# Attention on one core: GpSimd's background work at the end of a head step, memory terms two pieces later, reciprocals in two parts

## The chip, the core and the metric

One Trainium2 chip; the kernel runs on one of its cores. The metric is the device time of one execution in microseconds. Three runs of the kernel before took 708.51, 709.81 and 711.28 us (median 709.81). The profiled execution took 709.86 us, with a span of 708.2 us from its first to its last instruction.

The names of engines: PE is TensorE (PEld its weight load), DVE is VectorE, ACT is ScalarE, POOL is GpSimd, SP is SyncE, which here only issues DMAs. Each engine works through its own instructions in the order in which the program lists them, so an instruction that waits holds back all that stand behind it on that engine.

## What is computed

Two independent halves, side by side in the output. Half B is a spectral filter (a two-dimensional FFT, a product with weights, the inverse FFT); the change doesn't touch it. Half A is attention over 4 segments of 512 tokens with 32 heads of width 18, each segment with its own softmax and with a memory of the segments before:

```python
for s in range(N):                       # N = 4 segments
    qs, ks, vs = q[:, :, s], k[:, :, s], v[:, :, s]
    logits = jnp.einsum("bhqd,bhkd->bhqk", qs, ks) * scale + mask
    p = _softmax(logits, axis=-1)
    a_dot = jnp.einsum("bhqk,bhkd->bhqd", p, vs)
    pq = phi(qs)
    num = jnp.einsum("bhld,bhde->bhle", pq, M)
    den = jnp.einsum("bhld,bhd->bhl", pq, z)[..., None] + 1e-6
    a_mem = num / den
    o = g * a_mem + (1.0 - g) * a_dot
    outs.append(o)
    M = M + jnp.einsum("bhld,bhle->bhde", phi(ks), vs)
    z = z + jnp.einsum("bhld->bhd", phi(ks))
# o of all segments, (S, D) @ wo
```

The scores are large, so the kernel works them with high precision: operands are split into high and low parts, and the row maxima are subtracted inside the matmul.

## The kernel before, in words

The program lists FFT, projections of q, k and v, and the inverse FFT first (to about 355 us); the rest, function `attention`, is what the change works in. The order of its instructions is written out by hand: Python generators are advanced a piece at a time, and each piece lists a few instructions.

**Head steps.** The main loop runs t = 0 to 132, and step t handles one head of one segment (128 heads in all). Eight steps share a stack of q and k (`Qs`, `Ks`, loaded by four DMAs each, `stack_dmas`); the q of stack n+2 is loaded from step 8n on. Step t lists `s1(t+11)`, three pieces that compute scores for the maxima of a head eleven steps ahead (PE L656, L669; DVE reads them from PSUM: L670 `mx`, L664 `junk`, three PSUM banks "s1"), and `s2(t)`, three pieces that compute the scores again with the maxima subtracted (PE L705, L709/L710, L714) and their exponentials on ACT (L706, L711, L715). Every second step has half a `pv` (PE L734), the product with v for a quad of four heads. At the last head of a quad, GpSimd sets the masked corners of the four heads' exponentials to zero (`sel`, POOL L719), and the `pv` of that quad, two steps later, needs them.

**Maxima of a quad.** `mpath(k+2)` starts at the end of step t with t%4 == 0: GpSimd splits the quad's 128 x 16 maxima into a high and a low part (`mh`, POOL L685, L686), PE transposes them in step t+1 (`mt`, L689, behind that step's `pv`), ACT copies them and sends them to `Qs` by a DMA.

**Background.** `run_bg(0)` early in a step and `run_bg(1.2)` later in it advance the generators in the list `bg`, one after the other; with the rate of 1.2 this makes six turns in five steps, so in every fifth step there are two. The list holds, in order: `late_setup` (loads the output weights `wo` in six parts through two buffers `ob`; ACT rounds the high part `woh`, GpSimd makes the low part `wol`, L628), and for each segment g = 1, 2, 3 then `mixed(g)`, a part of the output projection of the segment before (`oproj`, PE L877), `den(g+1)` and the rest of `oproj`. `later(k, f)` puts f at the end of a later step: with k = 1 it is listed at the end of the same step, behind the step's `mpath`, lanes and U copies.

**`mixed(g)`** interleaves two things over five tiles of heads, in the order `ORD`. `combine(g-1)` finishes the segment before: PE spreads the reciprocal row sums over the rows (`pb`, L854), DVE multiplies (L857, L859), for a segment with memory GpSimd adds the memory term (`am`, L860), ACT rounds the high part (`oh`, L839), and GpSimd makes the low part (`ol`, L844). From step 118 on DVE takes the place of GpSimd in both (`s.now>=117`). `mem1(g, t)` makes the memory term of segment g: PE `pn` (L807), ACT copies it into `am` (L809), and in the next turn PE `pb` with the reciprocal denominators (L813) and DVE's product (L814). Up to there all these matmuls write the one PSUM bank "post". `mem1` starts d = 4 turns behind `combine` (d = 5 for g = 3).

**Reciprocals.** `recip` runs in the `lane` list, one piece a step: load 128 x 128 row sums (or denominators), wait three steps, reciprocal on DVE (L760), one step later ACT and GpSimd split it into three bf16 parts (L762 to L766), then a store to and a load from DRAM on SP give the wide copy `rr` (or `rd`) that `pb` needs. It runs eight times: for the row sums `rD` of segments 0 to 2 and the denominators `dD` of segments 1 to 3 with `slack=2`, and twice at the end for segment 3 without slack.

**The end.** Behind step 132 a loop runs what is left of `bg` (the projection of segment 2) and, at its turns 3, 8 and 10, `last_tile` (PE L886, DVE L887) for segment 3; then comes the projection of segment 3 (`last_proj`, L906).

Of the kernel before, what the change touches and what calls it, by code (L numbers as in the profile page):

```python
# [5 lines left out]
F32=mybir.dt.float32; F32R=mybir.dt.float32r  # L6
# [381 lines left out]
class ATT:  # L388
# [222 lines left out]
    def late_setup(s,cp):  # L611

        nc,io=s.nc,s.io; q=[]
        s.sel=cp.tile([96,5,126],BF,name="sel",bufs=1); nc.gpsimd.dma_start(s.sel,io["sel"].rearrange("p (t m) -> p t m",t=5))
        s.woh=cp.tile([128,5,576],F32R,name="woh",bufs=1); s.wol=cp.tile([128,5,576],F32R,name="wol",bufs=1)
        for t in (0,1,2,3,5,4,6):
            if t: yield
            if t<6:
                x=cp.tile([128,576],F32,name="ob"); q.append((t,x))
                nc.sync.dma_start(x,io["wo"][:,576*t:576*t+576])  # L620
            yield
            if t!=5: yield
            if len(q)>(t<6):
                u,x=q.pop(0)
                if u==5: nc.scalar.copy(s.wol[64:96,4],x[64:96]); continue
                r=128 if u<4 else 72
                nc.scalar.copy(s.woh[:,u],x)
                nc.gpsimd.tensor_tensor(s.wol[:r,u],x[:r],s.woh[:r,u].bitcast(F32),op=OP.subtract)  # L628
        yield
        yield from s.gates()  # L630
    def stack_dmas(s,n,qk):
# [120 lines left out]
    def recip(s,src,dst,gate,eps,load,slack=0):  # L752
        nc=s.nc; tp=s.tp
        w=tp.tile([128,3,128],BF,name="rw",bufs=2); y=tp.tile([128,128],F32,name="ry",bufs=2)
        nc.sync.dma_start(y,src.rearrange("h (b c) -> (h b) c",b=4))
        yield
        yield
        yield
        if eps: nc.vector.tensor_scalar(y,y,1e-6,None,op0=OP.add)
        nc.vector.reciprocal(y,y)  # L760
        yield
        nc.scalar.activation(y,y,AF.Copy,scale=gate)  # L762
        nc.scalar.copy(w[:,0],y)
        nc.gpsimd.tensor_tensor(y,y,w[:,0],op=OP.subtract)
        nc.gpsimd.tensor_copy(w[:,1],y)
        nc.gpsimd.tensor_tensor(w[:,2],y,w[:,1],op=OP.subtract)  # L766
        for _ in range(slack): yield
        nc.sync.dma_start(bass.AP(tensor=dst.tensor,offset=dst.offset,ap=[[128,128],[32*512,3],[1,128]]),w)
        yield
        yield  # L770
        r=tp.tile([96,512],BF,name=load,bufs=1)
        nc.sync.dma_start(r,dst)
        s.rc[load]=r
        yield
# [42 lines left out]
    def mixed(s,g):  # L817

        c=s.combine(g-1)
        d=5 if g==3 else 4  # L820
        for i in range(5+d):
            next(c,None); yield
            if i>=d:
                for _ in s.mem1(g,ORD[i-d]): yield
# [4 lines left out]
    def combine(s,g):  # L829

        nc=s.nc; tp=s.tp; xs=s.ux
        s.oh=[None]*5; s.ol=[None]*5
        eng=lambda: nc.vector if s.now>=117 else nc.gpsimd
        yield
        yield
        def high(u):
            r=126 if u<4 else 72
            s.oh[u]=tp.tile([128,512],F32R,name="oh",bufs=5); s.ol[u]=tp.tile([128,512],F32R,name="ol",bufs=5)
            (nc.vector.tensor_copy if s.now>=119 else nc.scalar.copy)(s.oh[u][:r],s.am[u][:r])  # L839
        def low(u):  # L840
            r=126 if u<4 else 72
            A,B=s.oh[u],s.ol[u]
            l=B if u<4 else tp.tile([128,512],F32R,name="ol4",bufs=1)
            eng().tensor_tensor(l[:r],s.am[u][:r],A[:r].bitcast(F32),op=OP.subtract)  # L844
            if u==4:
                s.later(1,lambda: nc.sync.dma_start(B[:72].bitcast(F32),A[:72].bitcast(F32)))
                s.later(2,lambda: (nc.sync.dma_start(A[72:128].bitcast(F32),l[:56].bitcast(F32)),nc.sync.dma_start(B[72:88].bitcast(F32),l[56:72].bitcast(F32))))
        late=g==2
        for t in range(7+late):
            if t>1 and not late: high(ORD[t-2]); low(ORD[t-2])  # L850
            if t<5:
                i=t; t=ORD[t]; r=126 if t<4 else 72; x=xs[t]
                pb=s.post("pb")
                nc.tensor.matmul(pb[:r],s.sel[:,t,:r],s.rc["rr"],start=True,stop=True)  # L854
                if g==0:
                    s.am[t]=tp.tile([126,512],F32,name="am",bufs=5)
                    nc.vector.tensor_tensor(s.am[t][:r],x[:r],pb[:r],op=OP.mult)  # L857
                else:
                    nc.vector.tensor_tensor(x[:r],x[:r],pb[:r],op=OP.mult)  # L859
                    eng().tensor_tensor(s.am[t][:r],x[:r],s.am[t][:r],op=OP.add)  # L860
                t=i
                if t<2: s.later(1,lambda t=t: s.ux_load(g,ORD[t+3]))
            if late and 1<t<7: high(ORD[t-2])
            if late and t>2: low(ORD[t-3])
            yield
# [290 lines left out]
```

## Time and profile before

| What | us |
|---|---|
| median of three runs | 709.81 |
| profiled execution | 709.86 |
| its span | 708.2 |
| TensorE busy | 678.8 |
| DVE busy | 544.8 |
| ACT busy | 455.8 |
| GpSimd busy | 194.6 |
| GpSimd's masks, L719, 132 instructions | 78.5 |
| GpSimd's low parts of the weights, L628, 5 instructions, each | 1.41 |
| GpSimd's low parts `ol`, L844, 10 instructions, each | 1.27 |

A row of the profile names the line of the kernel, the engine, the operation, what it writes and reads, how often (x), and what ended the idle time of the engine before it (`<-`). A window row gives the length of a stretch, the busy time of PE, PEld, DVE, ACT and POOL in it with the number of instructions, the granted TensorE clock (1.00 is full), the share of the time in which the 16 DMA engines were busy, and GB/s. A PE that is busy need not be working at its peak rate.

### The profile page before, as it was taken

The page shows a single profiled execution, that of the slowest core. Times are in us where ns is not written, and L with a number is a line of the kernel's source. Part 1 is how long each engine was busy: PE and PEld are TensorE (multiplying, and loading weights), DVE is VectorE, ACT ScalarE, POOL GpSimd, SP SyncE. Part 2 cuts the span into 40 slices and gives each one's busy share as a digit, 9 for nine tenths or more (in the row PEclk, how much of TensorE's full clock was granted, in tenths as well). Part 3 has the DMA queues.
Part 4 walks back from the last instruction along what each step waited for, and adds up shares of the span by engine and source line. Part 5 has one row for each costly group of instructions (what it writes and reads, how often), then busy time and mean ns, then how long its engine had stood idle before and what let it go on. Part 6 is the DMA issues. An engine that isn't in the chain of part 4 may idle for free.

```text
span 708.2 us, 14408 instructions
## 1 busy us (share of the span) xinstructions
PE 678.8 (96%) x4991; PEld 501.3 (71%) x4991; DVE 544.8 (77%) x1258; ACT 455.8 (64%) x1004; POOL 194.6 (27%) x392
## 2 busy tenths in 40 slices
PE   4999999999999999999999899999999999998997
PEld 3999769879779879998954454445566445663587
DVE  4899969899699789797787787988657876567533
ACT  3777796585686484544388777777656776567421
POOL 3111000100200102665135333444233752235310
PEclk9999999999999999999999999999999999999999
DMA  9897355666384679999338976976766766442151
GB/s 328 256 305 202 115 141 187 186 185 202 100 250 156 178 196 311 202 240 267 100 114 210 190 163 143 207 182 167 154 129 181 182 166 154 92 122 65 29 164 74
DMA packets 71146, 123.80 MB, mean 175 GB/s; under 512 B 12184, under 2 KB 39174, under 8 KB 67482
## 3 DMA queue, kind: packets, MB, share of 16 engines
q1 hardware_dynamic: 64422, 106.89, 57.4%
q0 software_dynamic: 5632, 15.76, 8.2%
q8 instruction: 39, 0.64, 0.4%
q10 hardware_dynamic: 1020, 0.25, 0.2%
q14 instruction: 33, 0.27, 0.1%
HBM read 82.10 MB, written 39.81 MB: 172 GB/s over the span
## 4 chain that ended last, share of the span: by engine, by line
PE 68%; DMA 8%; ACT 4%; DVE 4%; POOL 2%; issue 2%; SPq 0%; ACTq 0%; DVEq 0%; POOLq 0%
PE pj L464 12%; PE pv L734 9%; PE s L656 9%; PE pjv L464 8%; PE po L877 6%; PE i L309 3%; PE i L298 3%; PE s L705 3%; PE s L709 2%; DMA yb<-yout 2%; PE pn L807 2%; PE s L669 2%; PE pm L532 2%; PE s L714 2%; DMA Ks<-qkD 1%
## 5 line engine op out<-in xcount | busy, mean ns | idle before, releaser
L664 DVE CUSTOM_DVE_ANT_0 junk<-s,x 128x512 bf16<-128x512 f32 x248 | 137.0, 552 | 58.0 <-PE s L656 52.6
L719 POOL TENSOR_SCALAR_AFFINE_SELECT P<-P 128x512 f32<-128x512 f32 (+2 forms) x132 | 78.5, 626 | 112.9 <-ACT P L706 104.1
L670 DVE TENSOR_REDUCE mx<-s 128x4 f32<-128x512 f32 x128 | 87.7, 685 | 5.6 <-PE s L669 3.7
L706 ACT ACTIVATE P<-s 128x512 f32<-128x512 f32 x128 | 77.7, 607 | 10.8 <-PE s L705 3.8
L734 PE MATMUL pv<-P,vs 128*32 128x512 f32 (+3 forms) x1024 | 82.5, 439 | 0.1
L715 ACT ACTIVATE P<-s 128x256 f32<-128x256 f32 x128 | 49.8, 389 | 46.1 <-PE s L714 45.7
L711 ACT ACTIVATE P<-s 128x512 f32<-128x512 f32 x128 | 77.4, 605 | 2.4 <-PE s L710 2.2
L656 PE MATMUL s<-Ks,Qs 108*128 108x384 bf16 (+3 forms) x256 | 69.1, 301 | 1.5 <-DMA ux<-uD 1.0
L734 PEld LDWEIGHTS pv<-P,vs 128*32 128x32 f32 x1024 | 26.9, 109 | 45.3 <-issue 35.1
L464 PE MATMUL pj<-x,wqkh 128*128 128x512 f32 x162 | 56.5, 409 | 0.0
L208 DVE TENSOR_TENSOR Z<-t,t 128x290 f32<-128x290 f32 (+1 forms) x96 | 48.4, 553 | 0.1
L656 PEld LDWEIGHTS <-Qs 108*128 108x128 bf16 x320 | 31.5, 98 | 23.5 <-issue 12.1
L208 DVE TENSOR_TENSOR t<-Z 128x580 f32<-128x580 f32 x64 | 46.1, 755 | 0.0
L669 PE MATMUL s<-tri,idb 128*128 128x128 bf16 x256 | 43.0, 219 | 0.0
L522 POOL MEMSET vt<- 128x32 f32 x16 | 2.3, 162 | 141.3 <-PE pm L532 119.5
L298 PE MATMUL i<-civ,Y 128*128 128x256 f32 (+1 forms) x288 | 39.3, 289 | 0.2 <-POOL Y L283 0.2
L298 PEld LDWEIGHTS i<-civ,Y 128*128 128x128 f32 (+1 forms) x288 | 36.5, 181 | 1.0 <-POOL Y L283 0.4
L309 PE MATMUL i<-itab,T 128*128 128x290 f32 (+1 forms) x224 | 36.7, 306 | 0.5 <-DVE yout L317 0.4
L464 PE MATMUL pj<-x,wqkl 128*128 128x512 f32 x90 | 35.6, 395 | 0.0
L464 PE MATMUL pj<-xh,wqkl 128*128 128x512 f32 x90 | 35.5, 395 | 0.0
L143 PE MATMUL f<-ftab,eh 128*128 128x290 f32 x128 | 25.3, 321 | 10.7 <-DMA ftab<-ftab 10.6
L464 PE MATMUL pj<-xh,wqkh 128*128 128x512 f32 x90 | 35.5, 395 | 0.0
(210 smaller groups left out, 1806.3 us busy)
## 6 DMA issues: line engine op xcount, KB each, us to landing
qkD<-sp SPq DMA_DIRECT2D x32, 384.0 KB
xin<-xb SPq DMA_DIRECT2D x16, 384.0 KB
cfw<-cfw POOLq DMA_DIRECT2D x16, 384.0 KB, 4.7
civ<-civ POOLq DMA_DIRECT2D x16, 384.0 KB, 9.0
vs<-vD SPq DMA_DIRECT2D x16, 330.0 KB
vD<-vt SPq DMA_DIRECT2D x16, 311.0 KB
W<-w SPq DMA_DIRECT2D x16, 290.0 KB
yb<-yout SPq DMA_DIRECT2D x16, 290.0 KB
```

The source lines that it names most:

```text
L208: v.tensor_tensor(o,a,b,op=op)
L298: nc.tensor.matmul(p[:m,k],Y[i][:,q,c*128:c*128+m],cc[:,hl,o:o+256],start=n==0,stop=n==5)
L309: nc.tensor.matmul(p,x,t,start=n==0,stop=n==6)
L464: s.nc.tensor.matmul(out,a,b,start=i==0,stop=i==len(L)-1)
L656: nc.tensor.matmul(out,Q[:108,h,128*i:128*i+128],K[:108,h,:128*(i+1)],start=True,stop=True)
L664: nc.vector.tensor_tensor_reduce(out=junk[:,:w],in0=src,in1=s.mask[:,512-w:],scale=1.0,scalar=-3.0e38, op0=OP.add,op1=OP.max,accum_out=s.m ...
L669: nc.tensor.matmul(pa[:,o+w-128:o+w],s.idb,s.tri,start=False,stop=True,skip_group_check=True)
L670: nc.vector.tensor_reduce(out=s.mx[k][:,hh],in_=pa.rearrange("p (b c) -> p b c",c=128),axis=mybir.AxisListType.X,op=OP.max)
L706: nc.scalar.activation(P[0][:,hh],p0,AF.Exp,scale=SC)
L711: nc.scalar.activation(P[1][:,hh],p1,AF.Exp,scale=SC)
L719: nc.gpsimd.affine_select(out=x[:,r],in_=x[:,r],pattern=[[0,r.stop-r.start],[1,128]],compare_op=OP.is_ge,fill=0.0,base=0,channel_multiplie ...
L734: nc.tensor.matmul(s.pvt[32*hh:32*hh+32,128*j:],vt[:,j,19*h:19*h+32],mv[0][:,hh,mv[1]],start=j==0,stop=j>1,skip_group_check=True)
```

## The change

Four places, all in half A:

1. `late_setup`: GpSimd's low part of an output weight is listed at the end of its step (`later(1, ...)`), and a `yield` follows, so that the generator takes one more turn for each of five parts.
2. `recip`: with slack, except for the row sums of segment 2, the reciprocal is made in two halves of 64 columns, with a step between them. What follows in `recip` comes one step later.
3. `mixed`: for g = 1 and 2, `mem1` starts 6 turns behind `combine` and no longer 4, so `mixed` takes 21 turns and no longer 19.
4. `combine`: GpSimd's addition of the memory term and its low part are listed at the end of the step, if the step is one in which a quad's maxima are split (t%4 == 0, which at that place is `s.now%4 == 3`), for segments 0 and 1.

```diff
                 nc.scalar.copy(s.woh[:,u],x)
-                nc.gpsimd.tensor_tensor(s.wol[:r,u],x[:r],s.woh[:r,u].bitcast(F32),op=OP.subtract)
+                s.later(1,lambda u=u,x=x,r=r: nc.gpsimd.tensor_tensor(s.wol[:r,u],x[:r],s.woh[:r,u].bitcast(F32),op=OP.subtract))
+                yield
...
         if eps: nc.vector.tensor_scalar(y,y,1e-6,None,op0=OP.add)
-        nc.vector.reciprocal(y,y)
+        if slack and src is not s.rD[2]:
+            nc.vector.reciprocal(y[:,:64],y[:,:64])
+            yield
+            nc.vector.reciprocal(y[:,64:],y[:,64:])
+        else: nc.vector.reciprocal(y,y)
...
         c=s.combine(g-1)
-        d=5 if g==3 else 4
+        d=5 if g==3 else 6
...
-            eng().tensor_tensor(l[:r],s.am[u][:r],A[:r].bitcast(F32),op=OP.subtract)
+            x=s.am[u]; f=lambda e=eng(): e.tensor_tensor(l[:r],x[:r],A[:r].bitcast(F32),op=OP.subtract)
+            f() if eng() is nc.vector or s.now%4<3 or g==2 else s.later(1,f)
...
-                    eng().tensor_tensor(s.am[t][:r],x[:r],s.am[t][:r],op=OP.add)
+                    f=lambda t=t,x=x,r=r,e=eng(): e.tensor_tensor(s.am[t][:r],x[:r],s.am[t][:r],op=OP.add)
+                    f() if eng() is nc.vector or s.now%4<3 or g==2 else s.later(1,f)
```

## The prediction

> **What bounds the kernel now.** I read the page first, then the windows of the attention stage, then the idle times of TensorE in order of time.
>
> ```profile
> span 708.2 us, 14408 instructions
> PE 678.8 (96%) x4991; PEld 501.3 (71%) x4991; DVE 544.8 (77%) x1258; ACT 455.8 (64%) x1004; POOL 194.6 (27%) x392
> 355.00:395.00 40.00, 37.43 (x336) 19.47 (x338) 33.39 (x98) 32.07 (x77) 18.42 (x31) 1.00 0.70 166
> 550.00:590.00 40.00, 38.42 (x313) 19.29 (x306) 32.00 (x93) 29.20 (x68) 23.81 (x34) 1.00 0.78 178
> 635.00:670.00 35.00, 32.25 (x265) 14.40 (x257) 23.49 (x48) 22.60 (x53) 15.88 (x28) 1.00 0.19 54
> ```
>
> The columns of a window are its length, the busy times of PE, PEld, DVE, ACT and POOL, the granted clock, the DMA share and GB/s. TensorE is busy in all but 29.4 us of 708.2, so nothing here can be worth more than a few per cent. The three stretches are the ones the change works in; together they hold 2.57 + 1.58 + 2.75 = 6.9 us of idle TensorE.
>
> More is lost than these idle times show, because a late matmul also stretches its neighbours. So I cut windows at the starts of successive L705 matmuls: each is one head step, and its length is the first column. The first three are quiet steps (with a maxima transpose and pv; short; with pv). Then a step with one memory matmul pair (pn), one with a broadcast (pb), one with half an output projection, and then steps that the change touches: 9, 13, 17, 44, 86, 89, 91, 116.
>
> ```profile
> 432.18:434.82 2.64, 2.64 (x28) 1.25 (x27) 2.13 (x9) 1.89 (x6) 0.42 (x2) 1.00 0.26 56
> 434.82:436.10 1.28, 1.28 (x14) 0.82 (x11) 1.20 (x4) 1.24 (x4) 0.00 (x0) 1.00 0.52 146
> 436.10:438.69 2.59, 2.59 (x30) 1.20 (x28) 2.11 (x8) 1.73 (x5) 1.39 (x3) 1.00 0.64 152
> 577.58:579.72 2.14, 2.14 (x16) 1.17 (x14) 1.68 (x6) 1.78 (x5) 0.98 (x1) 1.00 0.41 123
> 567.70:569.14 1.44, 1.44 (x14) 0.92 (x12) 1.24 (x4) 1.40 (x5) 0.00 (x0) 1.00 0.91 149
> 631.62:633.85 2.23, 2.23 (x20) 1.75 (x18) 1.73 (x6) 2.09 (x6) 0.64 (x1) 1.00 0.00 0
> 371.51:374.71 3.20, 2.82 (x30) 1.16 (x28) 2.37 (x10) 1.92 (x6) 2.54 (x6) 1.00 0.92 205
> 379.91:383.45 3.54, 3.03 (x29) 1.13 (x27) 2.31 (x10) 1.92 (x6) 2.88 (x7) 1.00 0.95 273
> 388.60:392.23 3.63, 2.81 (x30) 1.25 (x28) 2.36 (x10) 2.69 (x8) 2.19 (x4) 1.00 1.00 200
> 446.74:449.33 2.59, 1.56 (x13) 0.85 (x11) 2.45 (x7) 2.56 (x8) 1.90 (x5) 1.00 0.72 158
> 555.89:559.05 3.16, 2.56 (x16) 1.20 (x14) 2.49 (x8) 2.24 (x6) 2.84 (x3) 1.00 0.74 196
> 563.48:567.70 4.22, 3.76 (x32) 1.54 (x30) 2.87 (x11) 2.64 (x8) 2.87 (x4) 1.00 0.99 186
> 569.14:573.34 4.20, 3.87 (x33) 1.71 (x30) 3.06 (x10) 2.26 (x6) 2.43 (x2) 1.00 0.68 135
> 640.31:642.28 1.97, 1.47 (x11) 0.83 (x9) 1.95 (x5) 1.73 (x4) 1.42 (x3) 1.00 0.01 2
> ```
>
> So pn costs 2.14 - 1.28 = 0.86, pb 0.16, half a projection 0.95. What a step takes over its parts: step 9 3.20 - 2.64 = 0.56, step 13 0.90, step 17 0.99, step 44 2.59 - 1.28 = 1.31, step 86 3.16 - (1.28 + 0.86 + 0.16) = 0.86, step 89 4.22 - (2.64 + 0.86) = 0.72, step 91 4.20 - (2.59 + 0.86 + 0.16) = 0.59, step 116 1.97 - (1.28 + 2 x 0.16) = 0.37. What ended the idle time says whose they are:
>
> ```profile
> 391.71 0.23 PE L689 MATMUL mt<-idb,mh 128*128 128x128 bf16 x1 [0.82 <-POOL mh L686]
> 398.09 0.32 PE L656 MATMUL s<-x,Qs 108*128 108x384 bf16 x1 [0.95 <-DVE mg L664]
> 448.99 0.32 PE L656 MATMUL s<-Ks,Qs 108*128 108x384 bf16 x1 [1.03 <-DMA ux<-uD]
> 557.57 0.65 PE L807 MATMUL pn<-pq,Mst 72*72 72x512 f32 x1 [0.60 <-DVE ux L859]
> 567.18 0.23 PE L689 MATMUL mt<-idb,mh 128*128 128x128 bf16 x1 [0.46 <-POOL mh L686]
> 641.85 0.38 PE L854 MATMUL pb<-rr,sel 96*126 96x512 bf16 x1 [0.50 <-DVE ux L859]
> 644.89 0.23 PE L689 MATMUL mt<-idb,mh 128*128 128x128 bf16 x1 [0.44 <-POOL mh L686]
> 680.68 0.38 PE L886 MATMUL pb<-rr,sel 96*126 96x512 bf16 x1 [0.77 <-DVE ux L887]
> ```
>
> **The change part by part.** Counting the yields (the background gets six turns in five head steps) gives the order of every queue.
>
> (a) *Low parts of the output weights.* Same five instructions, issued at the step's end, one more turn each. On GpSimd now:
>
> ```profile
> 386.62 2.40 POOL L719 TENSOR_SCALAR_AFFINE_SELECT P<-P 128x512 f32<-128x512 f32 x4 [3.74 <-ACT P L706]
> 389.81 1.41 POOL L628 TENSOR_TENSOR wol<-ob,woh 72x576 fp32r<-72x576 f32 x1 [0.79 <-ACT woh L627]
> 391.16 0.20 POOL L685 CAST mh<-mg 128x16 bf16<-128x16 f32 x1
> ```
>
> The split of the maxima (mh) stands behind a 1.41 us low part that itself waits for ScalarE. Moved, they land in steps 5, 8, 11, 14 and 20; the splits of steps 8, 16 and 20 come ahead of theirs, and only step 11's stays between the masks and a split, issued earlier than step 16's was. That frees 0.56 + 0.90 + 0.99 = 2.45 us. But step 20's end waits for the next heads' Qs, which the matmul at 398.09 is the first to use (idle 0.95). The DMA engines at that time, the last of the four Qs parts on SP, and one weight load:
>
> ```profile
> 386.00:388.00 2.00, 2.00 (x27) 0.99 (x18) 1.65 (x6) 1.86 (x6) 1.38 (x3) 1.00 0.55 139
> 388.00:398.00 10.00, 8.33 (x77) 4.16 (x75) 8.18 (x28) 7.69 (x20) 4.78 (x9) 1.00 1.01 200
> 389.31 0.37 SPq L640 DMA_DIRECT2D Qs<-reD  x1
> ob<-wo SPq DMA_DIRECT2D x6, 288.0 KB
> ```
>
> From 388 to 398 the DMA engines are full (1.01). Issue can move earlier by the 1.46 us of steps 9 and 13, but only 0.9 us (45% of 386 to 388) was free; and the later turns put the last 288 KB weight load into step 16, among the four Qs parts: 0.295 MB at 200 GB/s = 1.47 us. (On SP it waits for step 14's low part, whose buffer it fills; behind it stand three Qs parts and the pq loads.) TensorE leaves step 20 between 0.9 earlier and 1.47 - 0.9 = 0.57 later. I take -0.2, about the middle: the DMA engines, not the split, end that wait.
>
> [...]
>
> (b) *Reciprocals in two parts*, five of eight, with a step between.
>
> ```profile
> 447.45 0.95 DVE L760 RECIPROCAL ry<-ry 128x128 f32<-128x128 f32 x1
> 448.31 0.63 DVE L670 TENSOR_REDUCE mx<-s 128x4 f32<-128x512 f32 x1
> L608 DVE RECIPROCAL gt<-bt x1: 163/163/163, 393.8 to 393.8; 128x1 f32<-128x1 f32 x1
> ```
>
> One column takes 0.163 us and 128 take 0.95, so half takes 0.16 + 63 x (0.95 - 0.163)/127 = 0.55. The matmul at 448.99 needs the PSUM bank that mx still reads, until 448.31 + 0.63 = 448.94, and mx stands behind the two whole reciprocals of steps 43 and 44. That is step 44's 1.31, though the view names a DMA that landed then. Two halves come with step 43, one each with 42 and 44. Ahead of that mx stand three halves, 1.65, for 1.90: 0.25 less, 0.47 if halves cost half. I take -0.4; bounds 0 and -1.3 (all of it). In the later stages projections hide the reciprocals: step 112, with half a projection, holds DVE 1.73 us of 2.23. If that cover went, five splits would cost 5 x 0.15 = 0.75. The stores and loads of the split reciprocals on SP come a step later, and so do their first users: the three steps between stay.
>
> [...]
>
> (c) *Memory terms two pieces later, first stage (steps 52 to 67).* The doubled turn at step 56 again holds a pb and a pn on the one "post" bank, so that wait stays. Two later pb's lose their neighbour: -0.3, between 0 and -0.9.
>
> (d) *Second stage (85 to 100).* Gone: 0.86 + 0.72 + 0.59 = 2.17. New: step 86 holds two pb's, the second behind DVE's product of the first, as in step 116 (idle 0.50) but with more maxima work on DVE, 0.5 to 1.1. And GpSimd:
>
> ```profile
> L844 POOL TENSOR_TENSOR ol<-am,oh 126x512 fp32r<-126x512 f32 (+1 forms) x10 | 12.7, 1273 | 16.1 <-ACT oh L839 15.2 <-PE pn L807 0.9
> L860 POOL TENSOR_TENSOR am<-ux,am 126x512 f32<-126x512 f32 (+1 forms) x8 | 10.1, 1271 | 2.9 <-DVE ux L859 2.9
> ```
>
> From step 85's end to step 87 six of these, 6 x 1.27 = 7.6, and three masks, 3 x 0.6 = 1.8, must pass before pv of step 89: 9.4 us. TensorE gets there in 1.28 + 2.59 + 1.28 + 4 x 0.16 + 0.7 = 6.5, where 0.7 is about half a short step ahead of pv, plus some 1 us that DVE holds the two pb's of step 86 and 1 us from the pb of step 85 to the first am (both estimates from the idles 0.50 and 0.60 behind that product): 8.5. Stall about 1; none if DVE holds it longer, 2.2 if it doesn't. So 2.17 less 0.8 less 1.1: -0.2, from -1.3 to +1.1. Deferral puts step 88's split ahead of its low part; that is the 0.46 at 567.18.
>
> (e) *Step 116* loses both pb's, and its split goes first: these are 0.37 and the 0.44 at 644.89. I take -0.9, a little over their sum, as ScalarE's two high parts move later too; 0 to -1.3. The denominators' wide copy is now issued at step 118 and used in 121.
>
> (f) *The end.* The background is two projection halves behind, while one pn and pb moved past the last head: TensorE reaches the second last_tile 2 x 0.95 - 1.02 = 0.88 earlier against its ux load, so the 0.77 at 680.68 grows. +0.4; 0 to +0.9.
>
> Sum: -0.2 - 0.4 - 0.3 - 0.2 - 0.9 + 0.4 = -1.6. The profiled execution took 709.86 (span 708.2 and 1.7 around it), the median of the runs is 709.81: 708.3.
>
> **Rivals.** *All the waits go* (704.3). The Qs land before they are needed (-1.5 for -0.2), step 44 is free (-1.3), stages -0.6 and -1.3, step 116 -1.3, end +0.4: -5.6. For it: every wait above ends on work that is moved. Against: the DMA share of 1.01.
>
> [...]
>
> *GpSimd becomes the bound* (712.5). Each low part waits for its high part on ScalarE: 15.2 us in 10 instructions, 1.5 each. Two such waits ahead of the masks make 9.4 + 3.0 = 12.4 against 8.5 minus the hold: pv of step 89 waits 4 to 5 instead of 1 and step 57's about 1 likewise. -1.6 + 3.5 + 0.7 = +2.6. It decides once the masks of step 87 start over 2 us after their exponentials. Against: the ScalarE wait overlaps am's work, which I counted.
>
> **How the numbers follow.** Forecast 0.42, own range 706.0 to 711.0; all waits go 0.34; weight load 0.11; GpSimd 0.13. Half a per cent is 3.5 us, about what a measurement of this kernel can tell from no change: faster means under 706.3, slower over 713.4. Faster: 0.30 of the 0.34 and 0.05 of the forecast, 0.35. Slower: 0.07 of GpSimd's and 0.02 of the rest, 0.09. The range reaches to 703.9 and 712.0.
>
> **What would show it.** The transposes L689 of steps 9, 13, 17, 89 and 117 without idle time before them; the wait at step 20's end longer than 0.95 (a), gone if all waits go; halves of 0.5 us and step 44 about 0.4 shorter (b); in step 86 an L854 behind DVE L859, in step 89 pv behind POOL L719, by 1 us or by 4 (d); step 116 at 1.28 (e); the idle before the second last_tile over 0.77 (f). A loss ahead of 355 us or in the projections would make it wrong altogether.

## The result and the profile after

The changed kernel takes 713.93 us (median of 6 runs, 712.57 to 715.76) where the kernel before takes 709.54 in the same comparison: ratio 1.0066, 95% interval 1.0046 to 1.0085. Two more comparisons gave 1.0059 (1.0038 to 1.0081) and 1.0054 (1.0034 to 1.0074). It is slower by some 4 us; 708.3 was forecast, and 712.0 was the end of the range. The profiled execution took 713.58, its span 711.9.

The line numbers of the changed kernel are one higher from L629 on (L705/L706 are now L706/L707, L734 is L735), five higher behind the reciprocals and more from `combine` on (L854 is L860, L886 is L893). One row of the list of TensorE's waits before, then four of the changed kernel's (total us, times, longest):

```profile
PE mt L689 <- POOL mh L686: 2.7, 6, 0.8
```

```profile
PE s L706 <- ACT P L707: 4.3, 7, 2.9
PE pb L893 <- DMA rr<-rrD: 1.5, 1, 1.5
PE pv L735 <- issue: 0.7, 1, 0.7
PE mt L690 <- POOL mh L687: 0.2, 1, 0.2
```

TensorE's wait for the split maxima has shrunk from 2.7 to 0.2 us, so the change did what it says there. But a wait of 2.9 us for ScalarE's exponentials is new, and at the end one of 1.5 for the reciprocals `rr`. The windows of the changed kernel, cut as before (steps 9, 13 and 17; then 19, 20 and 21; then 86, 89 and 116):

```profile
372.55:375.19 2.64, 2.64 (x30) 1.26 (x28) 2.24 (x9) 2.48 (x7) 1.08 (x3) 1.00 1.01 189
380.34:382.98 2.64, 2.64 (x30) 1.25 (x28) 2.24 (x9) 1.91 (x6) 1.45 (x3) 1.00 0.87 167
388.13:390.77 2.64, 2.64 (x30) 1.25 (x28) 2.24 (x9) 2.58 (x7) 1.19 (x4) 1.00 0.96 166
392.05:397.70 5.65, 2.75 (x29) 1.24 (x27) 2.99 (x10) 1.15 (x4) 0.00 (x0) 0.99 1.02 184
397.70:400.54 2.84, 2.46 (x10) 1.12 (x10) 1.21 (x5) 2.82 (x7) 2.40 (x4) 0.50 0.91 169
400.54:404.95 4.41, 4.41 (x30) 1.62 (x29) 1.70 (x4) 1.84 (x7) 1.78 (x3) 0.56 0.79 206
559.14:561.77 2.63, 1.91 (x15) 1.12 (x13) 2.63 (x8) 2.22 (x6) 2.02 (x2) 1.00 0.18 58
566.37:570.94 4.57, 3.83 (x32) 1.44 (x30) 2.75 (x10) 2.13 (x6) 4.49 (x8) 1.00 1.01 217
644.21:645.55 1.34, 1.04 (x9) 0.55 (x7) 1.32 (x4) 1.34 (x5) 1.01 (x2) 1.00 0.32 127
```

Steps 19, 20 and 21 of the kernel before:

```profile
393.51:396.10 2.59, 2.59 (x29) 1.20 (x27) 2.38 (x11) 1.26 (x4) 0.09 (x1) 1.00 0.97 169
396.10:398.43 2.33, 1.38 (x14) 0.75 (x12) 2.01 (x8) 2.33 (x7) 2.31 (x4) 1.00 0.98 198
398.43:401.03 2.60, 2.60 (x31) 1.26 (x29) 1.61 (x4) 1.33 (x5) 0.42 (x2) 1.00 0.94 187
```

Steps 9, 13 and 17 last 2.64, a quiet step: the 2.45 us are freed to the hundredth. Steps 19, 20 and 21 then take 12.9 us where they took 7.5. In step 21 nothing is idle, but the granted clock is 0.56, and 30 matmuls last 4.41 where 31 took 2.60. Why TensorE stands in step 19 is seen on ScalarE, first in the changed kernel, then in the kernel before (start, length, what ended the idle time):

```profile
392.16 0.39 ACT L716 ACTIVATE P<-s 128x256 f32<-128x256 f32 x1
396.38 0.62 ACTq L696 DMA_DIRECT2D x<-mts  x1
397.05 0.60 ACT L707 ACTIVATE P<-s 128x512 f32<-128x512 f32 x1 [4.50 <-DMA pq<-pqD]
```

```profile
393.62 0.39 ACT L715 ACTIVATE P<-s 128x256 f32<-128x256 f32 x1
394.67 0.62 ACTq L695 DMA_DIRECT2D x<-mts  x1
395.34 0.60 ACT L706 ACTIVATE P<-s 128x512 f32<-128x512 f32 x1 [1.33 <-DMA pq<-pqD]
```

ScalarE has an 8 KB DMA to issue (the transposed maxima), and every later exponential stands behind it. The issue comes 3.8 us after ScalarE is free (396.38 - 392.55); before it came 0.7 after (394.67 - 394.01). The profile puts the end of both waits on the landing of a 252 KB `pq` load from SP's queue, which has nothing to do with the maxima. What joins the two is a number: in the trace the landings of the DMAs of SP and ScalarE are counted on eight semaphores in turn, and these two have the same one (109 in both kernels). In both kernels, in e3 and in p1 below the issue comes 0.07 to 0.08 us after the last DMA of that number has landed (in p1 it is a `Qs` load). ScalarE arrives 1.46 us earlier in the changed kernel, but the load, issued at 388.05 (388.06 before), lands at 396.31 instead of 394.60. Step 0 itself starts 1.02 us later in the changed kernel's profile; measured from there, ScalarE arrives 2.5 us earlier and the load lands 0.7 later.

The stages, from the starts of L706's matmuls (L705 before), one profiled execution each:

| us | steps 0-23 | 24-47 | 48-79 | 80-111 | 112-126 | 127 to the end |
|---|---|---|---|---|---|---|
| before | 49.71 | 50.85 | 86.90 | 88.89 | 30.60 | 45.93 |
| after | 52.52 | 50.29 | 84.34 | 89.13 | 33.04 | 46.24 |
| after, second profile (e9) | 51.09 | 50.28 | 84.87 | 89.13 | 33.03 | 49.03 |
| after, third profile (e13) | 50.23 | 50.98 | 85.12 | 89.11 | 33.03 | 46.12 |

Three projection halves (2.85 us) moved from the third column to the fifth, and one memory pair (0.86; the broadcasts are 7 behind step 127 in both) from the fifth to the last. Net of them the profiled change costs +2.8, -0.6, +0.3, +0.2, +0.4 and -0.5; the rest of the 3.7 us in span (+1.0) lies ahead of step 0, where the two kernels are the same. That part is not the same from profile to profile: step 0 starts at 354.69 us in e10's (see below), at 355.27 in that of the kernel before and at 356.29 here. So the last column and the first have to be read over several.

### The profile page after: what moved, and what is told of

Same layout as the page of the kernel before. It is cut to its first block, busy times and chain, and to the rows that moved or that the text cites. A ratio compares the mean times of both kernels' runs of the same rounds, so it can differ in the third digit from the quotient of the medians.

```text
span 711.9 us, 14430 instructions
## 1 busy us (share of the span) xinstructions
PE 679.7 (95%) x4991; PEld 501.5 (70%) x4991; DVE 548.5 (77%) x1267; ACT 454.2 (64%) x1002; POOL 193.8 (27%) x390
## 4 chain that ended last, share of the span: by engine, by line
PE 78%; DMA 9%; ACT 4%; DVE 3%; POOL 3%; issue 2%; ACTq 0%; SPq 0%; POOLq 0%; DVEq 0%
PE pj L464 14%; PE pv L735 10%; PE s L657 10%; PE pjv L464 7%; PE po L884 6%; PE f L143 4%; DMA yb<-yout 4%; PE c L163 4%; PE s L706 3%; PE i L309 3%; PE s L710 3%; PE i L298 2%; PE po L913 2%; PE pn L812 2%; PE s L670 2%
## 5 line engine op out<-in xcount | busy, mean ns | idle before, releaser
L707 ACT ACTIVATE P<-s 128x512 f32<-128x512 f32 x128 | 77.8, 608 | 12.8 <-PE s L706 4.9
L735 PE MATMUL pv<-P,vs 128*32 128x512 f32 (+3 forms) x1024 | 83.5, 443 | 1.4 <-issue 0.7
L735 PEld LDWEIGHTS pv<-P,vs 128*32 128x32 f32 x1024 | 27.0, 110 | 48.7 <-issue 37.9
L208 DVE TENSOR_TENSOR t<-Z 128x580 f32<-128x580 f32 x64 | 46.1, 757 | 0.0
L298 PE MATMUL i<-civ,Y 128*128 128x256 f32 (+1 forms) x288 | 39.3, 289 | 0.2 <-POOL Y L283 0.2
```

What stands on the lines that cost most here:

```text
L208: v.tensor_tensor(o,a,b,op=op)
L298: nc.tensor.matmul(p[:m,k],Y[i][:,q,c*128:c*128+m],cc[:,hl,o:o+256],start=n==0,stop=n==5)
L707: nc.scalar.activation(P[0][:,hh],p0,AF.Exp,scale=SC)
L735: nc.tensor.matmul(s.pvt[32*hh:32*hh+32,128*j:],vt[:,j,19*h:19*h+32],mv[0][:,hh,mv[1]],start=j==0,stop=j>1,skip_group_check=True)
```

## Experiments: which part loses

**The parts and the whole.** The weights edit undone (e1, and again as e11), and alone (e2, again as e12):

```diff
-                s.later(1,lambda u=u,x=x,r=r: nc.gpsimd.tensor_tensor(s.wol[:r,u],x[:r],s.woh[:r,u].bitcast(F32),op=OP.subtract))
-                yield
+                nc.gpsimd.tensor_tensor(s.wol[:r,u],x[:r],s.woh[:r,u].bitcast(F32),op=OP.subtract)
```

> The changed kernel with only the edit of the output weights' low parts undone (GpSimd's instruction back in its place, no additional turn). Theory: the loss is all in that edit. In head step 18 ScalarE issues a small DMA that has to wait until an earlier transfer has landed; the changed kernel has one more 288 KB load ahead of it, ScalarE stands for 3.8 us, TensorE for 2.9 us, and its granted clock falls to 0.5 for 6.8 us. Then this kernel has no clock drop and takes 707 to 710 us, the same as before. Rival: the loss is in the memory terms two pieces later, where GpSimd's masks come late for pv of step 89 and projection halves are pushed behind; then this kernel stays at 712 to 716.

> The kernel before with the weights edit alone (low parts as background steps of their own, a step later). Theory: the loss is this edit's by itself: it frees some 2.4 us in steps 9, 13 and 17, arrives at step 20 while the DMA engines are still full, stops there for 3 us or more, and the clock falls to 0.5. Expected 712 to 715 us, a profile with 0.5 near 397 us and an end from step 127 as before (45.9 us). Rival: the weights edit does harm only together with the rest of the change; then 707 to 711 us and the clock stays at 1.0 until the last microseconds.

e1: 711.59, ratio 1.0017 (0.9996 to 1.0039), between its two forecasts, with the clock at 1.0 through steps 16 to 24 of the profile. e2: 710.65, 1.0010 (0.9994 to 1.0026): the theory's 712 to 715 was wrong. It does lose the clock: in 11 of its 12 executions the mean granted clock is 0.994 to 0.997, and only 5 of the 34 of the kernel before beside them are as low; the time that it frees pays for that. So neither part alone made the whole loss, and the two were measured again beside the whole:

> The changed kernel once more, beside the three below. Theory: its loss comes from the stop at steps 19 to 21 and the clock behind it, and both come in nearly every execution: 712.5 to 715.5 us, a mean granted clock of 0.994 to 0.996 in most of the runs where the kernel before has 0.998 to 1.0. Rival: the stop is a matter of chance in the DMA engines, as the smaller losses of the weights edit alone and of the rest alone suggest; then 710.5 to 712.5 us, with single runs at 0.998 and more.

> The changed kernel with the weights edit undone, once more, beside the next two and the kernel before. Theory: the rest of the change costs +0.7 us in the stages from step 24 on and 0 to +1 at the end, net of the work moved: ratio 1.001 to 1.0025. Rival: nothing, 0.999 to 1.001.

> The kernel before with the weights edit alone, once more. Theory: the stop at steps 19 to 21 is made by this edit, in its own way in each execution (step 24 begins 49.2 to 52.5 us behind step 0, before 49.7): ratio 1.001 to 1.004, mean granted clock 0.994 to 0.997 in most runs. Rival: the edit alone costs nothing and the loss needs the rest of the change: ratio 0.998 to 1.001.

> The changed kernel, in the same comparison as the two runs before. Theory: its ratio is the sum of the two others' losses within the intervals, 1.003 to 1.006. Rival: 1.006 or more with the two others together under 0.003: then the parts work on each other in a way that is not shown by the stages.

e9: 713.65. In one comparison e11 gave 1.0029 (1.0008 to 1.0050), e12 1.0008 (0.9986 to 1.0029) and e13 1.0054 (1.0034 to 1.0074). e11 is above its forecast and e12 just below its own, in the range of its rival. The parts add up to 0.37%, inside the whole's interval: a plain sum is not contradicted, and no working of the parts on each other is shown. So there are two losses to find: the weights edit frees 2.45 us and ends at nothing or worse, and the rest, forecast at -1.4, costs 1.2 (e1) to 2.1 us (e11).

**Is it the late weight load?** The low parts put off, but without the extra turn, so that the weight loads stay in their old steps:

```diff
                 s.later(1,lambda u=u,x=x,r=r: nc.gpsimd.tensor_tensor(s.wol[:r,u],x[:r],s.woh[:r,u].bitcast(F32),op=OP.subtract))
-                yield
```

> The changed kernel with GpSimd's low parts of the output weights still at the step's end, but without the additional turn, so that the weight loads come at their old steps. Theory: the late loads are what costs, and the order on GpSimd is what gains: the transposes of steps 9, 13 and 17 keep part of their 2.4 us, no clock drop, 705 to 708 us. Rival (the low parts at the step's end cost by themselves, since SP's next load waits for them): 711 to 715 us.

715.63, ratio 1.0066 (1.0041 to 1.0091): the theory failed, and the time is just over the rival's. All weight loads are issued by 380.2 us here, and ScalarE stands longest of all:

```profile
397.04 0.60 ACT L706 ACTIVATE P<-s 128x512 f32<-128x512 f32 x1 [6.21 <-DMA pq<-pqD]
```

Its `pq` load, issued at 386.2, lands 10.1 us later. The late weight load is not needed for the stop.

**Is it ScalarE's small DMA?** That one DMA issued by GpSimd instead, which also lists it a step earlier:

```diff
-        if s.now<0: nc.gpsimd.dma_start(out,mt)
+        if s.now<0 or k==6: nc.gpsimd.dma_start(out,mt)
```

> The changed kernel; only the small DMA of one quad's maxima (quad 6, issued by ScalarE in step 18) is issued by GpSimd, so that a wait for an earlier transfer holds back GpSimd and not ScalarE's exponentials. Theory: ScalarE's stop is what makes TensorE idle; without it the wait for Qs at the end of step 20 remains, 1 to 3 us, and the clock stays at 1.00 or falls later: 708 to 711 us. Rival (TensorE waits for the stack loads in any case, as long as those come late): 712 to 715 us with the idle time moved to the end of step 20.

714.13, ratio 1.0046 (1.0029 to 1.0062), as the rival had it. ScalarE no longer stands, but TensorE does, at the end of step 20, where the next heads' Qs are first used:

```profile
396.26 0.32 PE L657 MATMUL s<-x,Qs 108*128 108x384 bf16 x1 [3.19 <-DMA pq<-pqD]
```

The profile names a `pq` load; the last part of Qs, which this matmul reads, landed 0.2 us ahead of it, at 396.06. So the small DMA decides where the time is lost, not that it is.

**What does the clock add?** 14 matmuls of 96x512 whose result nobody uses, in step 20:

```diff
+            if t==20:
+                wm=s.post("wm")
+                for _ in range(14): nc.tensor.matmul(wm,s.idb[:96],s.sel.rearrange("p t m -> p (t m)")[:,:512],start=True,stop=True)
```

> The changed kernel with 14 matmuls of 96 x 512 whose result is not used, listed in step 20 ahead of the matmul that waits for ScalarE, into a PSUM bank that is free there: 14 x 0.22 = 3.0 us of work inside an idle time of 2.9 us. Theory: half of the loss is the clock that falls to 0.5 for 6.8 us after the idle time; with TensorE kept busy it stays at 1.00, steps 21 and 22 take 2.6 and 1.3 us, and the time falls by 1.5 to 2.5 us, to 711.5 to 712.5. Rival (steps 21 to 23 are long because of late masks and exponentials, not because of the clock): 713.5 to 716.

711.91, ratio 1.0026 (1.0005 to 1.0048). Steps 19 (its window holds the 14 matmuls), 20 and 21 now:

```profile
389.48:395.85 6.37, 5.78 (x44) 2.57 (x42) 2.98 (x10) 1.15 (x4) 0.00 (x0) 1.00 1.00 205
395.85:397.59 1.74, 1.42 (x10) 0.74 (x10) 0.97 (x3) 1.74 (x5) 1.72 (x3) 1.00 0.94 197
397.59:400.29 2.70, 2.70 (x30) 1.25 (x28) 1.90 (x8) 2.68 (x8) 1.66 (x5) 1.00 0.91 192
```

Work that does nothing wins back about 0.3% (from separate comparisons), as forecast: in the profile the stop in step 19 stays, but the clock is at 1.00 and step 21 takes 2.70, not 4.41.

**Is it the full DMA engines?** The five `pq` loads (1.18 MB, 5.9 us at the 200 GB/s that the DMA engines moved from 388 to 398 before) go from steps 16 to 20 to steps 0 to 4, in the changed kernel (e6), in the kernel before (e7), and in the kernel before with the weights edit (e10, again as e15):

```diff
-            if 16<=t<21: s.pq_load(1,ORD[t-16])
+            if t<5: s.pq_load(1,ORD[t])
```

> The changed kernel, but the five loads pq of the second piece (1.2 MB in all) issued at steps 0 to 4, where the DMA engines are a quarter to half busy, instead of steps 16 to 20, where they are full. Theory: the stop in steps 19 and 20 comes from the queue on the DMA engines; without these loads the Qs land some 4 us sooner, no wait is left at the end of step 20, the clock stays at 1.0 and the 2.4 us of steps 9, 13 and 17 are kept: 705 to 708.5 us. Rival: ScalarE's stop and the wait are due to the late weight load or to the order of the queues whatever is behind; then 712 to 715 us.

> The kernel before, with the same move of the pq loads to steps 0 to 4 and nothing else. Theory: it loses only the idle 0.95 us at the end of step 20, so 708.5 to 710 us, within measurement of no change; the difference from the changed kernel with the same move is then what the change gives where the DMA engines do not stop it, -1 to -4 us. Rival: the move alone gains 3 us or more, and the change itself gives nothing.

> The kernel before with the weights edit and with the pq loads at steps 0 to 4; reciprocals, memory terms and combine as before. Theory: the weights edit gives its 2.4 us where the DMA engines are not full, and nothing takes them back: step 24 begins 46.2 us behind step 0 as in the changed kernel with early pq loads (49.7 before), the rest as before: 704.5 to 706.5 us, ratio 0.992 to 0.996, below the kernel before with early pq loads alone (0.997). Rival: whatever arrives earlier is lost again at the next group of heads (steps 43 to 45) to the next burst of loads; then 707 to 709 us.

> The kernel before with early pq loads and the weights edit once more, beside the run with the split: 704 to 707 us, ratio 0.991 to 0.996, as in the first comparison. Rival: the first value was luck; 0.996 to 0.999.

e7: 707.95, ratio 0.9968 (0.9952 to 0.9984), a little more gain than the theory gave it. e10: **705.32, ratio 0.9932 (0.9908 to 0.9956)**, and e15 706.27, 0.9943 (0.9922 to 0.9964): faster than both kernels. e6: 708.24, 0.9977 (0.9956 to 0.9998). All but e7 are within their forecasts; but with the loads early the whole change gives nothing (e6 against e7), where e7's forecast had 1 to 4 us. In e10 the stretch of the full DMA engines, then steps 19, 20 and 21:

```profile
388.00:398.00 10.00, 9.89 (x98) 5.24 (x91) 8.53 (x27) 8.89 (x22) 4.22 (x8) 1.00 0.95 190
390.45:393.03 2.58, 2.58 (x29) 1.19 (x27) 2.10 (x8) 1.72 (x5) 1.38 (x3) 1.00 0.99 162
393.03:394.52 1.49, 1.38 (x13) 0.75 (x11) 1.47 (x5) 1.49 (x4) 1.01 (x2) 1.00 0.99 165
394.52:397.12 2.60, 2.60 (x31) 1.26 (x29) 2.04 (x8) 2.48 (x8) 1.10 (x3) 1.00 0.82 188
```

TensorE is busy 9.89 of the 10 us (8.33 before). Steps 0 to 23 take 46.29 us in e10 and 46.19 in e6, 48.90 in e7 and 49.71 before: with the `pq` loads out of the queue the weights edit gives 2.6 us (48.90 - 46.29), with them in it nothing. The DMA engines are nearly as busy as before (0.95 against 1.01, and 0.99 in steps 19 and 20 against 0.97 and 0.98), so a high DMA share by itself isn't the cost. What changed is what stands ahead of the needed loads: the last part of Qs lands 39.3 us behind step 0 in e10, 42.6 before and 42.5 to 43.5 in the three profiles of the changed kernel. ScalarE's small DMA now has the number of a store issued 11 us earlier, and in e6, e7 and e10 it is issued while ScalarE is still busy with the exponentials ahead of it, so it holds nothing back. That settles its half: what takes the 2.45 us is the queue on the DMA engines, by ScalarE's issue or by the Qs, whichever comes first.

## Experiments: the rest of the change

All but e8 are the kernel before with early `pq` loads and one part; e14 has the weights edit too, and p3 the edits of p2. p1, p2 and p3 were run once each, so only their profiles are read.

**Reciprocals in two parts**, as in the change:

> The kernel before with the pq loads at steps 0 to 4 (so that the stretch is not disturbed by full DMA engines) and the reciprocals in two parts, nothing else. Read from the profile, stage by stage against the same kernel without the split. Prediction's term: steps 24 to 48 shorter by 0.4 us, bounds 0 and 1.3. Theory now: 0.0 to 0.3 shorter there, since what step 44 gains comes back in step 45 or 49, and no difference above 0.1 us behind step 48.

> The kernel before with early pq loads, the weights edit and the reciprocals in two parts; memory terms and combine as before. Theory: the split gains nothing: what steps 43 and 44 save (0.3 to 0.4) comes back in steps 45 and 49 (0.4), and the loads of the reciprocals rr, a step later, leave the first combine broadcast (then in step 52) under 0.9 us of slack where it had 1.9, so some executions wait there: ratio to the kernel before 0.993 to 0.996, that is 0 to 0.2% above the same kernel without the split. Prediction's term: 0.4 us, 0.06%, below it.

p1 took 708.77 in its one run and missed its expectation: steps 24 to 47 took 52.96, not 50.1 to 50.4, because ScalarE's small DMA of step 43 stood in the next full queue (ScalarE idle for 3.00 us; from 440 to 450 the DMA share was 0.94 before and 0.97 after) and TensorE behind it:

```profile
445.06 0.38 PE L705 MATMUL s<-Qs,Ks 110*128 110x512 bf16 x1 [1.40 <-ACT P L706]
```

e14, beside e15, was not disturbed: 0.9941 (0.9919 to 0.9963) against 0.9943 without the split, which can't tell 0.4 us (0.06%) from nothing. In the profile step 44 is 0.37 shorter than in e10, steps 45 and 49 are 0.22 and 0.17 longer: nothing is left there. Behind step 48 there are differences that neither the prediction nor p1's expectation had: the extra turn moves one projection half from steps 48 to 79 to step 113, and net of it 48 to 79 are 1.4 us longer than in e10, 80 to 111 0.8 shorter, and the end 1.0 shorter (there by the wait at the second `last_tile`, which varies from profile to profile: 0.8 before, 0.2 after, 1.1 in e10). The halves last what was worked out, and the wait behind them stays (changed kernel):

```profile
448.23 0.55 DVE L762 RECIPROCAL ry<-ry 128x64 f32<-128x64 f32 x1
451.98 0.32 PE L657 MATMUL s<-Ks,Qs 108*128 108x384 bf16 x1 [1.04 <-DVE mx L671]
```

**Memory terms two pieces later** (p2), **and GpSimd's combine put off as well** (p3):

```diff
-        d=5 if g==3 else 4
+        d=5 if g==3 else 6
```

> The kernel before with the pq loads at steps 0 to 4 and the memory terms two pieces later, nothing else. By stages, net of the matmuls that move from one step to another (memory pair 0.86, broadcast 0.16, half a projection 0.95). Prediction's terms c, d and f: 48 to 80 -0.3, 80 to 112 -0.2 to 0, the end +0.4. Theory now: this part is what costs in the stages, 48 to 80 +0.2 to +0.4 and 80 to 112 +0.1 to +0.6 (without the deferral the masks come later still), and at the end TensorE stands 1.5 to 2 us at the first last_tile, because two projection halves less (1.9 us) and one memory pair more (0.86) stand ahead of it while the reciprocals land 12.1 us behind step 127's start as before.

> As the run before, with GpSimd's combine instructions at a step's end put off by a step as well. Prediction's terms d and e: against the run with the memory terms alone step 88 to 89 gains 0.4 or more and steps 116 and 117 about 0.9 together. Theory now: the steps from 112 on lose as much as they gain (step 125 by 0.7 to 0.9), by the memory terms, not by the putting off; then the run before shows step 125's loss too. Rival: the putting off makes step 125's idle time; then the run before lacks it.

p2 took 709.94. It takes 85.31 us in steps 48 to 79 (86.90 in e7; 0.3 more net of two projection halves, as expected) and 90.37 in steps 80 to 111 (88.88 in e7): 1.5 more where 0.1 to 0.6 was expected. The masks are what its step 89 waits for:

```profile
555.59 0.38 PE L854 MATMUL pb<-rr,sel 96*126 96x512 bf16 x1 [0.60 <-DVE ux L859]
563.60 1.60 PE L734 MATMUL pv<-P,vs 128*32 128x512 f32 x16 [1.53 <-POOL P L719]
```

From 112 to 126 p2 and p3 are equal to 0.01 us in every step: the putting off is for segments 0 and 1 and cannot reach these steps, which my rival had overlooked; p3's theory held there. What is won and lost there is the memory terms' doing, as theirs is 32.47 against 30.58 (two halves more, 1.90, and one pair less, 0.86: 0.85 worse than even). In steps 80 to 111 p3, which took 717.25, was worse than p2 (93.54), where a gain of 0.4 in steps 88 and 89 was expected: a 1.08 us idle in step 88 behind DVE, and the clock at 0.5 for 6.83 us from 562.2. Only with the reciprocals' extra turn, in the whole change, does this stage cost 0.2 (89.11 to 89.14 us in all nine profiles that hold the whole rest of the change).

**The end.** In these nine profiles (after, e1, e3 to e6, e9, e11, e13) TensorE stands 1.2 to 2.2 us at the first `last_tile` for `rr`; in the eight without the later memory terms it never does. The changed kernel's row:

```profile
678.02 0.38 PE L893 MATMUL pb<-rr,sel 96*126 96x512 bf16 x1 [1.50 <-DMA rr<-rrD]
```

`rr` lands 12.0 to 13.0 us after step 127's start in all of them. Ahead of the first `last_tile` there were 42 projection matmuls and one memory pair, and there are 28 and two: 1.9 us less and 0.86 more. From step 127 on the nine take 46.1 to 49.9 us, 48.0 in the mean; the eight 44.9 to 47.4, mean 45.9. Of the 2.1 between them 0.86 is the pair moved there, 1.2 is lost. The later memory terms alone don't make the whole of that wait: in p2 and p3 35 projection matmuls stand ahead, and TensorE stands 0.49 and 0.66, not the 1.5 to 2 expected of p2; the second half is moved by the reciprocals' extra turn. The first `last_tile` one turn later, in e6:

```diff
-            if i in (3,8,10): s.last_tile((3,8,10).index(i),"rr")
-            if i==3: s.ux_load(3,3)
+            if i in (4,8,10): s.last_tile((4,8,10).index(i),"rr")
+            if i==4: s.ux_load(3,3)
```

> The changed kernel with the pq loads at steps 0 to 4, and the first last_tile one turn of the background later (turn 4 for turn 3, its ux load with it). Theory on the end: in the changed kernel TensorE stands 1.5 to 2.2 us at the first last_tile for the reciprocals rr, 0 before, because half a projection less of work stands ahead of it; one turn more (half an output projection, 0.95 us, or a quarter) hides half or all of it: 0.5 to 1.5 us less than the run with only the pq loads moved. Rival: the next last_tile then waits as much more for its ux load (idle 0.2 to 1.8 there now): no difference.

709.22, ratio 0.9998 (0.9977 to 1.0019), no better than e6: the rival was right, the wait moved to the second `last_tile`.

```profile
672.51 0.38 PE L893 MATMUL pb<-rr,sel 96*126 96x512 bf16 x1 [0.37 <-DMA rr<-rrD]
679.12 0.38 PE L893 MATMUL pb<-rr,sel 96*126 96x512 bf16 x1 [2.52 <-DVE ux L894]
```

## Why the prediction was wrong

**(a) is the step that failed first.** Its gross 2.45 came in exactly, and so did its reason that the DMA engines "end that wait". Wrong was the price, "TensorE leaves step 20 between 0.9 earlier and 0.57 later". Measured from step 0 it left step 20 at 43.16 us before and at 44.25, 43.78 and 43.26 in the three profiles of the changed kernel: 1.09, 0.62 and 0.10 later. The last part of Qs was to be issued up to 1.46 earlier; it was issued 0.0, 0.5 and 1.0 earlier, and landed 9.4 us after its issue in all three, 8.6 before. Two terms were missing. ScalarE's small DMA, which the sum left out, stood 3.8 us (3.2 to 4.1 in the three profiles, 0.7 before), with the exponentials of two steps behind it. And the clock fell at the stop, which the sum had nowhere: steps 21 to 23 took 8.27, 7.31 and 6.97 us, 6.55 before. In all, steps 0 to 23 took 50.23 to 52.52 us, 49.71 before, 48.95 and 49.31 with the edit undone (e1, e11). The case to which the weight load's 0.11 was given, step 20 ending the 0.57 late of (a), had the right place and a wrong cause: e3 loses as much with the weight loads early.

The loads whose place counted were others than the weight load that (a) weighed: the `pq` loads issued early gain 0.3% by themselves (e7) and open the weights edit's gain (e10).

**(b)** -0.4 was forecast, nothing came in its steps: the halves cost 0.55 as worked out, but step 44 gained 0.37 and steps 45 and 49 gave back 0.39 (e14).

**(c) and (d)** were given -0.5 together and cost +0.5 in the profile (+0.3 and +0.2). The mechanisms of (d) were as described: step 86 waits 0.72 behind DVE, step 89's pv 0.63 for the masks (about 1 was forecast), step 91 is 0.7 shorter. It was the balance of gains and new waits that came out on the other side. That the stage costs 0.2 and not the 1.5 of p2 is luck: the prediction gave the reciprocals' turn no part in it. The waits of the changed kernel, in steps 86 and 89 and then in step 125 for (e):

```profile
560.99 0.38 PE L860 MATMUL pb<-rr,sel 96*126 96x512 bf16 x1 [0.72 <-DVE ux L865]
567.87 1.60 PE L735 MATMUL pv<-P,vs 128*32 128x512 f32 x16 [0.63 <-POOL P L720]
662.64 1.28 PE L735 MATMUL pv<-P,vs 128*32 128x512 f32 x16 [0.68 <-issue]
```

**(e)** Steps 116 and 117 are 0.99 shorter (0.9 was forecast), and 0.32 of it is the two broadcasts that left. But the work that was put off stands in later steps now and costs more there than it saved: steps 112 to 126 take 33.04 where 30.60 + 2.85 - 0.86 = 32.59 would be even, so +0.4 in place of -0.9. In step 125, for one, pv comes behind 0.68 us in which the profile shows no wait. I added up what the step loses and forgot to ask where its work would stand.

**(f)** The size, net of the moved work, was 0.4 and is 1.2 over the profiles (-0.5 in the changed kernel's first). The place was wrong: the first `last_tile` waits, for `rr`. The second's wait for its `ux` did not grow: 0.9 in the mean of the nine profiles and of the eight.

**The sum.** The rest of the change was forecast at -1.4 and measures about +2 (e1 +0.2%, e11 +0.3%; e6 against e10 +0.45%, from two comparisons), the weights edit at -0.2 and measures +0.6 (e12, whose interval of -1.0 to +2.1 holds the forecast too) to +2 (steps 0 to 23: 51.28 in the mean of the three profiles above, 49.32 in the mean of before, e1 and e11). So by size the larger part of the miss is in the rest: 1.3 in (e), 1.0 in (c) and (d), 0.8 in (f) and 0.4 in (b). GpSimd did not become the bound; that rival's step 89 waits 0.63 and not 4.

How the loss splits exactly between the two halves stays open within their intervals. So does why the `pq` load that ScalarE's issue waits for takes 6.5 us in one execution and 10.1 in another.

## What to carry to other kernels

Before counting a freed wait as gained, ask what TensorE runs into next. If that is a queue of loads, move loads that are not urgent out of it first: here the same edit is worth nothing with the `pq` loads in the queue and 2.6 us without them. An engine that issues even an 8 KB DMA between its compute instructions can share the fate of the queue, as ScalarE did here (3.8 us). And work that is put off has to be followed to where it lands, with what covers it there; at the end of this kernel it ate 1.2 us of the cover of the last chain.

## What the runs showed of the hardware

In these runs a stop of TensorE could cost more than its length. After 2.9 us of idle time the granted clock was 0.5 for 6.83 us (after), after 2.30 and 3.19 us for 3.41 (e13, e4), and after three idles of 0.7, 0.2 and 1.1 us, whose ends lie 6.0 us apart, for 6.83 (p3). After 1.40 us in p1 it was 0.5 for 3.41, after 1.41 in e2 and 2.52 in e8 it stayed at 1.0, so the length of one idle time alone doesn't decide. What does is not shown.

Such stops came in other crowded stretches too (DMA share 1.05 and 0.99 in the 9 to 10 us ahead of these): e6's profile stood 2.02 us at the first broadcast of step 52 for `rr`, e15's 2.36 in step 51, each with the clock at 0.5 at it or behind it.

```profile
462.11 0.58 PE L860 MATMUL pb<-rr,sel 96*72 96x512 bf16 x1 [2.02 <-DMA rr<-rrD]
```
